# Block-sparse attention in 64-query blocks, with probabilities as weights of v and a planned order of all engines

## The chip, the cores and the metric

The kernel runs on one core of a Trainium2 chip. The metric is the device time of one launch in microseconds (us); lower is better. Engines are named as in the profile: PE is the matrix engine (PEld its weight loads), DVE the vector engine, ACT the scalar engine, POOL the GpSimd engine that issues the loads, SP the engine that issues the stores. PE reads from the on-chip memory and writes only to PSUM, which has eight banks of 512 float32 columns on 128 partitions; ACT and DVE move results out of it.

## The reference

Two parts follow each other. The first is attention over q, k and v of shape (4 batches, 8 heads, 768 positions, 64). Each query sees the keys less than 16 positions away, and besides them 24 summaries: for each block of 32 keys the elementwise maximum of k, with the mean of v as its value and log 32 added to its score.

```
scores_l = scale * q @ k^T          # kept where |i - j| < 16
scores_s = scale * q @ k_sum^T + log(32)
a = softmax([scores_l, scores_s]);  attn = a @ [v, v_sum]
```

The second part is a feed-forward network on the 3072 rows of the heads joined (512 wide): `h = x @ w_in` (512 to 2048), `g = h * clip(h + 3, 0, 6) / 6`, `out = g @ w_out` (2048 to 512). Inputs and output are float32; both kernels convert inputs to bf16 on load.

## The kernel before

**Tiles.** The 3072 rows are cut into eight tiles of 384 rows: half of a batch each. Heads are taken in four pairs p. For each tile, `F1` (L382) makes one 128-wide slice of h: four matmuls of 384 columns into the PSUM tile `hp` (L389), a Relu on ACT with the bias tile `half_c` (L392) and a DVE operation that makes `g` (L393); there are 16 slices. `F2` (L395) accumulates 16 matmuls of 512 columns per 128 rows (L402), copies the result on ACT (L406) and stores it from SP (L408).

**Attention by pair.** `Tk` and `Tq` (L264, L298) transpose k and q. Batches 0 and 1 are loaded as runs of eight rows (four for batch 0's q) and transposed by matmuls with a 64-wide output on half of the columns of the array (L271, L312); batches 2 and 3 come in natural order and take six 128-wide transposes per pair (L274, L305). Copies spread k into the block-diagonal tile `kbd` (two heads at once, 64 keys of each). `Sl` (L316) makes scores for 12 key blocks, each against 94 queries (L321), with Exp on ACT (L324) and a mask multiplication on DVE (L325). `Ss` (L327) makes the scores of the summaries (L331, L334). `AV` (L348) multiplies by v with the probabilities as the moving operand (L357, L359), makes the denominators with four more matmuls against a matrix of ones (L363 to L373), takes the reciprocal as Ln and Exp on ACT (L375, L376) and multiplies on DVE (L377); its result is already the transposed x that F1 reads. The block means of v come from an own load of v in float32, `vr`, added up on DVE (`vsum`, L229); for batch 0 from matmuls `vps` (L252) and a transfer `vs` on SP (L259).

**What sets the order.** POOL issues the loads in program order. Up to the first `AV`s of batch 0, PE, ACT and DVE also follow the program. Afterwards a table of slots (L451 to L501) puts the pieces of attention between the slices of the feed-forward part: one slot is one slice of F1 and three matmuls of F2 of the tile before. The work list (L503) runs F1 of tile 0 alone, then F1(1) with F2(0), F2(1) alone, F1(2) alone, F1(t) with F2(t-1) for t from 3 to 7, and F2(7) alone. The loads of batch 1 are held back until slice 11 of tile 0 exists (L490). PSUM: two banks each for `h`, `o` and `s`, and one each for `num` and `den`.

Of the kernel before, what the change touches and what calls it, by code (L numbers as in the profile page):

```python
# [14 lines left out]
ET = mybir.EngineType  # L15
# [3 lines left out]
KB = 64  # L19
HALO = 15  # L20
WIN = KB + 2 * HALO
HALF = 384
NLONG = 2
RUN = 8
PCS = 4
RP = 96
QCUT = 480
# [3 lines left out]
def kernel(  # L31
# [13 lines left out]
    NT = S // 128  # L45
    NK = S // KB
# [5 lines left out]
    RS = 4 * NB  # L52
# [3 lines left out]
    work = ctx.enter_context(tc.tile_pool(name="work", bufs=2))  # L56
    xp = ctx.enter_context(tc.tile_pool(name="xp", bufs=4))
    gp = ctx.enter_context(tc.tile_pool(name="gp", bufs=3))
    hw = ctx.enter_context(tc.tile_pool(name="hw", bufs=3))
    PS = bass.MemoryType.PSUM  # L60
    ps_h = ctx.enter_context(tc.tile_pool(name="ps_h", bufs=2, space=PS))
    ps_o = ctx.enter_context(tc.tile_pool(name="ps_o", bufs=2, space=PS))
    ps_s = ctx.enter_context(tc.tile_pool(name="ps_s", bufs=2, space=PS))
    ps_n = ctx.enter_context(tc.tile_pool(name="ps_n", bufs=1, space=PS))

    nc.scalar.preload_act_table_set("natural_log_exp_and_others")


    kbd = [const.tile([128, NK, 128], BF16, tag=f"kbd{p}", name=f"kbd{p}") for p in range(NP)]
    vall = const.tile([128, NP, NK, 128], BF16, tag="vbd", name="vbd")  # L70
    vbd = [vall[:, p] for p in range(NP)]
    qT = [const.tile([128, S + 2 * HALO + 2], BF16, tag=f"qT{p}", name=f"qT{p}") for p in range(NP)]
    at = [const.tile([128, NK, WIN], BF16, tag=f"at{p}", name=f"at{p}") for p in range(NP)]
    kst = [const.tile([128, RS], BF16, tag=f"kst{p}", name=f"kst{p}") for p in range(NP)]
    vst = [const.tile([RS, 2, D], BF16, tag=f"vst{p}", name=f"vst{p}") for p in range(NP)]
    w_in_sb = const.tile([128, NP, d_ff], BF16, tag="win", name="win")
    w_out_sb = const.tile([128, NFT, d_model], BF16, tag="wout", name="wout")


    kb_t, qb_t, vr_t, vf = {}, {}, {}, {}  # L80

    def load_k(b, p, n=1):

        if b < NLONG:
            t = ld.tile([RP, 2 * n, RUN, D], BF16, tag=f"kb{n}", name="kb", bufs=2)
            nc.gpsimd.dma_start(out=t[:], in_=k[b, 2 * p:2 * p + 2 * n].rearrange("h (p s) d -> p h s d", s=RUN))
        else:
            t = ld.tile([128, NT, 2, D], BF16, tag="kb", name="kb")
            load_natural(t, k, b, p)
        for i in range(n):  # L90
            kb_t[b, p + i] = t, i

    def load_q(b, p, n=1, part=None):

        if b < NLONG:
            lo, hi, r = cut(part)
            t = ld.tile([(hi - lo) // r, 2 * n, r, D], BF16, tag=f"qb{n}", name="qb", bufs=1 if n == 4 else 2)
            nc.gpsimd.dma_start(
                out=t[:], in_=q[b, 2 * p:2 * p + 2 * n, lo:hi].rearrange("h (p s) d -> p h s d", s=r))
        else:  # L100
            t = ld.tile([128, NT, 2, D], BF16, tag="qb", name="qb")
            load_natural(t, q, b, p)
        for i in range(n):
            qb_t[b, p + i, part] = t, i

    def cut(part):
        return {None: (0, S, RUN), 0: (0, QCUT, RUN // 2), 1: (QCUT, S, RUN // 2)}[part]

    def load_natural(t, src, b, p):
        for j in range(2):  # L110
            nc.gpsimd.dma_start(out=t[:, :, j], in_=src[b, 2 * p + j].rearrange("(s p) d -> p s d", p=128))  # L111

    def load_v(b, g, lo=0, hi=NK):

        for p in (2 * g, 2 * g + 1):
            for j in range(2):
                rows = slice(64 * j, 64 * j + 64)
                nc.gpsimd.dma_start(out=vall[rows, p, lo:hi, rows],  # L118
                                    in_=v[b, 2 * p + j].rearrange("(n k) d -> k n d", k=KB)[:, lo:hi])

    def load_vf(p):

        if not vf:
            t = gp.tile([128, NP, NK, D], F32, tag="g", name="vf")
            vf.update({i: t[:, i] for i in range(NP)})
        for j in range(2):
            nc.gpsimd.dma_start(out=vf[p][64 * j:64 * j + 64],  # L127
                                in_=v[0, 2 * p + j].rearrange("(n k) d -> k n d", k=KB))

    def load_vrows(b, g):  # L130

        w = BLK // PCS * D
        vr_t[b, g] = ld.tile([RS, PCS, w + 8], F32, tag="vr", name="vr", bufs=2)
        nc.gpsimd.dma_start(out=vr_t[b, g][:, :, 0:w],
                            in_=v[b, 4 * g:4 * g + 4].rearrange("h (n c t) d -> (h n) c (t d)", c=PCS, n=NB))

# [3 lines left out]
    def load_w_in(c):  # L140
        w = d_ff // 4
        nc.gpsimd.dma_start(out=w_in_sb[:, :, c * w:(c + 1) * w], in_=w_in_v[:, :, c * w:(c + 1) * w])

    def load_w_out(c):
        w = NFT // 4
        nc.gpsimd.dma_start(out=w_out_sb[:, c * w:(c + 1) * w], in_=w_out_v[:, c * w:(c + 1) * w])


    ctx.enter_context(tc.manual_schedule(engines={ET.Pool}))
    start = tc.manual_schedule(engines={ET.PE, ET.Activation, ET.DVE})  # L150
    start.__enter__()
    load_vf(0)
    ident = const.tile([128, 128], BF16, tag="id", name="ident")
    nc.gpsimd.memset(ident[:], 1.0)
    nc.gpsimd.affine_select(out=ident[:], in_=ident[:], compare_op=ALU.is_equal, fill=0.0, base=0,
                            channel_multiplier=1, pattern=[[-1, 128]])
    load_vf(1)
    load_k(0, 0)
    load_q(0, 0, 1, 0)
    load_vf(2)  # L160


    mask = const.tile([128, WIN], BF16, tag="mask", name="mask")
    nc.gpsimd.memset(mask[:], 1.0)
    for j in range(2):
        m = mask[j * 64:(j + 1) * 64]
        nc.gpsimd.affine_select(out=m, in_=m, compare_op=ALU.is_ge, fill=0.0, base=0,
                                channel_multiplier=-1, pattern=[[1, WIN]])
        nc.gpsimd.affine_select(out=m, in_=m, compare_op=ALU.is_ge, fill=0.0, base=2 * HALO,
                                channel_multiplier=1, pattern=[[-1, WIN]])  # L170
    load_vf(3)
    load_k(0, 1)
    load_q(0, 1, 1, 0)
    load_k(0, 2, 2)
    load_q(0, 2, 2, 0)


    hm4 = const.tile([RS, 4, D], F32, tag="hm4", name="hm4")
    osum4 = const.tile([RS, 4, D], BF16, tag="osum4", name="osum4")
    nc.gpsimd.memset(hm4[:], 1.0)  # L180
    nc.gpsimd.affine_select(out=hm4[:], in_=hm4[:], compare_op=ALU.is_ge, fill=0.0, base=0,
                            channel_multiplier=1, pattern=[[-NB, 4], [0, D]])
    nc.gpsimd.affine_select(out=hm4[:], in_=hm4[:], compare_op=ALU.is_ge, fill=0.0, base=NB - 1,
                            channel_multiplier=-1, pattern=[[NB, 4], [0, D]])
    hmv = [hm4[:, 2 * par:2 * par + 2] for par in range(2)]
    osum = [osum4[:, 2 * par:2 * par + 2] for par in range(2)]
    obd = const.tile([128, 2, D], BF16, tag="obd", name="obd")
    hmk = const.tile([128, 2, NB], BF16, tag="hmk", name="hmk")
    half_c = const.tile([128, 1], F32, tag="half", name="half_c")
    zero = const.tile([128, 1], F32, tag="zero", name="zero")  # L190
    nc.vector.memset(zero[:], 0.0)

    def zero_off_diagonal(eng, t):
        w = t.rearrange("p n c -> p (n c)").bitcast(F32).rearrange("p (n c) -> p n c", c=64)
        for r, c in ((slice(0, 64), slice(32, 64)), (slice(64, 128), slice(0, 32))):
            if eng is nc.scalar:
                eng.copy(w[r, :, c], zero[r].unsqueeze(2).to_broadcast([64, NK, 32]))
            else:
                eng.memset(w[r, :, c], 0.0)


    ind = const.tile([128, 2, 2, 4], F32, tag="ind", name="ind")
    nc.vector.memset(ind[:], 0.0)
    for i in range(4):
        for par in range(2):
            nc.vector.memset(ind[32 * i:32 * i + 32, par, par, i:i + 1], 1.0)
    for p in range(NP):
        zero_off_diagonal(nc.vector if p < 2 else nc.scalar, kbd[p][:])
    NK0 = 7
    load_w_in(0)  # L210

    def zero_rest():
# [4 lines left out]
        for t in (hmk, obd):  # L217
            nc.vector.memset(t[:], 0.0)
            nc.vector.memset(t[0:64, 0], 1.0)
            nc.vector.memset(t[64:128, 1], 1.0)  # L220
# [324 lines left out]
```

## Time and profile before

| | |
|---|---|
| median of three runs (lowest, highest) | 266.62 us (264.75, 266.89) |
| span of the profiled execution, first to last instruction | 262.8 us |
| what lies outside that span, against the median | 3.8 us |
| busy PE, ACT, DVE, POOL | 238.0, 169.3, 154.2, 72.5 us |
| first matmul of F1; last matmul of F2 | 34.85 us; 258.77 us |
| mean granted PE clock | 0.973 |

The profile is of one execution. For that execution it gives the span alone; its time is taken as the span and the 3.8 us that separate it from the median. A row of a group gives busy time and the mean of one instruction; the duration of a matmul contains a latency that overlaps with the next one, so the pace of matmuls is read from the distance of starts in the timeline or in the chain.

### The profile page before, as it was taken

The page shows a single profiled execution, that of the slowest core. Times are in us where ns is not written, and L with a number is a line of the kernel's source. Part 1 is how long each engine was busy: PE and PEld are TensorE (multiplying, and loading weights), DVE is VectorE, ACT ScalarE, POOL GpSimd, SP SyncE. Part 2 cuts the span into 40 slices and gives each one's busy share as a digit, 9 for nine tenths or more (in the row PEclk, how much of TensorE's full clock was granted, in tenths as well). Part 3 has the DMA queues.
Part 4 walks back from the last instruction along what each step waited for, and adds up shares of the span by engine and source line. Part 5 has one row for each costly group of instructions (what it writes and reads, how often), then busy time and mean ns, then how long its engine had stood idle before and what let it go on. Part 6 is the DMA issues. An engine that isn't in the chain of part 4 may idle for free.

```text
span 262.8 us, 4842 instructions
## 1 busy us (share of the span) xinstructions
PE 238.0 (91%) x1848; PEld 135.9 (52%) x1872; DVE 154.2 (59%) x360; ACT 169.3 (64%) x327; POOL 72.5 (28%) x104
## 2 busy tenths in 40 slices
PE   0946899999899969999899999999999999999993
PEld 0215556644455636666455556566655555555541
DVE  3594556632889774998994566668534544444400
ACT  7665578842587867998586567757766555555410
POOL 8994000566273600796920310000000000000000
PEclk9995599999999999999999999999999999999999
DMA  3999994299999971899990551001011111101122
GB/s 111 178 155 201 206 206 76 37 204 209 203 255 118 180 80 44 58 130 187 185 145 19 54 70 44 36 7 40 2 40 40 42 40 40 40 2 41 40 82 80
DMA packets 57848, 25.80 MB, mean 98 GB/s; under 512 B 45281, under 2 KB 53217, under 8 KB 57825
## 3 DMA queue, kind: packets, MB, share of 16 engines
q0 software_dynamic: 54160, 19.14, 63.5%
q1 hardware_dynamic: 3664, 6.34, 6.5%
q8 instruction: 15, 0.25, 0.4%
q14 instruction: 9, 0.07, 0.1%
HBM read 31.98 MB, written 6.29 MB: 146 GB/s over the span
## 4 chain that ended last, share of the span: by engine, by line
PE 62%; DMA 11%; DVE 8%; ACT 7%; POOL 7%; issue 3%; ACTq 0%; POOLq 0%
PE op L402 24%; PE hp L389 24%; DMA vr<-in_v_dram 8%; POOL vbd L118 3%; PE num L359 2%; DMA vs<-vs 2%; PE sl L321 2%; POOL vf L127 2%; DVE g L393 2%; PE num L357 2%; PE ss L331 2%; ACT kbd L281 2%; PE den L363 1%; PE den L366 1%; DMA vf<-in_v_dram 1%
## 5 line engine op out<-in xcount | busy, mean ns | idle before, releaser
L389 PE MATMUL hp<-x,win 128*128 128x384 bf16 x512 | 104.1, 326 | 2.8 <-DVE g L393 2.4
L392 ACT ACTIVATE r<-hp,half_c 128x384 f32<-128x384 f32 x128 | 73.5, 580 | 45.8 <-PE hp L389 45.0
L402 PE MATMUL op<-wout,g 128*128 128x512 bf16 x360 | 96.2, 379 | 1.1 <-issue 0.2
L393 DVE SCALAR_TENSOR_TENSOR g<-r,hp 128x384 bf16<-128x384 f32 x128 | 69.6, 551 | 45.6 <-ACT r L392 45.4
L389 PEld LDWEIGHTS <-win 128*128 128x128 bf16 x512 | 47.3, 98 | 37.2 <-issue 6.0
L402 PEld LDWEIGHTS <-g 128*128 128x128 bf16 x384 | 36.8, 98 | 32.8 <-issue 0.5
L377 DVE TENSOR_TENSOR x<-num,lg 128x384 bf16<-128x384 f32 x32 | 17.7, 555 | 24.7 <-ACT lg L376 22.8
L118 POOL DMA_DIRECT2D vbd<-in_v_dram x24 | 18.2, 775 | 37.7 <-PE num L359 33.6
L375 ACT ACTIVATE lg<-den 128x384 f32<-128x384 f32 x32 | 15.7, 492 | 16.0 <-PE den L373 7.4
L324 ACT ACTIVATE at<-sl 128x376 bf16<-128x376 f32 (+2 forms) x48 | 22.4, 490 | 2.3 <-PE sl L321 2.3
L406 ACT COPY ot<-op 128x512 f32<-128x512 f32 x24 | 13.9, 583 | 8.9 <-PE op L402 8.8
L325 DVE TENSOR_TENSOR at<-at,mask 128x376 bf16<-128x376 bf16 (+2 forms) x48 | 16.2, 349 | 3.6 <-ACT at L324 3.4
L359 PEld LDWEIGHTS <-vbd 128*128 128x128 bf16 x224 | 13.8, 102 | 8.0 <-issue 4.5
L376 ACT ACTIVATE lg<-lg 128x384 f32<-128x384 f32 x32 | 16.8, 526 | 0.8
L321 PE MATMUL sl<-qT,kbd 128*128 128x94 bf16 x192 | 15.0, 214 | 1.9 <-ACT at L324 0.8
L321 PEld LDWEIGHTS <-kbd 128*128 128x128 bf16 x192 | 12.2, 102 | 7.7 <-issue 1.8
L359 PE MATMUL num<-at,vbd 128*128 128x94 bf16 (+2 forms) x224 | 15.0, 206 | 0.0
L111 POOL DMA_DIRECT2D qb<-in_q_dram x16 | 13.5, 861 | 4.8 <-DMA vr<-in_v_dram 4.8
L252 PE MATMUL vps<-vf,ind 128*8 128x384 f32 x16 | 7.5, 612 | 7.6 <-DMA vf<-in_v_dram 7.6
L111 POOL DMA_DIRECT2D kb<-in_k_dram x16 | 13.5, 865 | 0.0
L357 PE MATMUL num<-asum,vst 96*128 96x384 bf16 x32 | 11.0, 344 | 2.6 <-DVE x L377 2.2
L281 ACT COPY kbd<-tp 64x768 bf16<-64x768 bf16 x12 | 9.5, 792 | 5.2 <-PE tp L271 5.1
(82 smaller groups left out, 219.8 us busy)
## 6 DMA issues: line engine op xcount, KB each, us to landing
out_dram<-ot SPq DMA_DIRECT2D x24, 256.0 KB, 2.0
vr<-in_v_dram POOLq DMA_DIRECT2D x6, 768.0 KB, 7.7
vbd<-in_v_dram POOLq DMA_DIRECT2D x24, 96.0 KB, 3.9
win<-in_moe_w_in_dram POOLq DMA_DIRECT2D x4, 512.0 KB, 11.1
wout<-in_moe_w_out_dram POOLq DMA_DIRECT2D x4, 512.0 KB, 18.3
vf<-in_v_dram POOLq DMA_DIRECT2D x8, 192.0 KB, 3.7
kb<-in_k_dram POOLq DMA_DIRECT2D x16, 96.0 KB, 6.8
qb<-in_q_dram POOLq DMA_DIRECT2D x16, 96.0 KB, 6.4
```

Of the source, the lines that this page charges most:

```text
L111: nc.gpsimd.dma_start(out=t[:, :, j], in_=src[b, 2 * p + j].rearrange("(s p) d -> p s d", p=128))
L118: nc.gpsimd.dma_start(out=vall[rows, p, lo:hi, rows], in_=v[b, 2 * p + j].rearrange("(n k) d -> k n d", k=KB)[:, lo:hi])
L321: nc.tensor.matmul(sp[:, i * WIN:(i + 1) * WIN], kbd[p][:, t], qT[p][:, t * KB:t * KB + WIN], start=True, stop=True)
L324: nc.scalar.activation(a, sp[:, 0:n * WIN].rearrange("p (n c) -> p n c", c=WIN), AF.Exp, scale=scl)
L357: nc.tensor.matmul(num[:], vst[p][:].rearrange("p h d -> p (h d)"), asm[:], start=True, stop=False)
L359: nc.tensor.matmul(num[:, lo:hi], vbd[p][:, t], a[:, t, off:off + hi - lo], start=False, stop=(i == len(bl) - 1))
L376: nc.scalar.activation(lg[:], lg[:], AF.Exp, scale=-1.0)
L377: nc.vector.tensor_tensor(xt[s][:, p], num[:], lg[:], op=ALU.mult)
L389: nc.tensor.matmul(hp[:], w_in_sb[:, kt, ft * 128:(ft + 1) * 128], xt[t][:, kt], start=(kt == 0), stop=(kt == NP - 1))
L392: nc.scalar.activation(r[:], hp[:], AF.Relu, bias=half_c[:], scale=1.0 / 6.0)
L393: nc.vector.scalar_tensor_tensor(gt[t][:, ft], r[:], 1.0, hp[:], op0=ALU.min, op1=ALU.mult)
L402: nc.tensor.matmul(op[:], gt[t][:, ft, ts * 128:(ts + 1) * 128], w_out_sb[:, ft], start=(ft == 0), stop=(ft == NFT - 1))
```

## The change

The attention part is written anew; the feed-forward part keeps its matmuls. By parts:

- **Scores.** A query block has 64 queries. Its keys stand in one tile `kaug` of 120 columns: 64 own keys, 16 to the right, 16 to the left, and 24 maxima. For each head, one matmul with 64 rows of weights (the head's 64 features, on partitions 0 to 63 or 64 to 127) makes the scores of all 120 keys against 64 queries: 12 matmuls per pair and half batch, the two heads into two banks of the PSUM tile `S` (new L378 to L396). One Exp over 120 x 768 and one mask multiplication over 96 x 768 follow.
- **Values.** The probabilities of 64 queries become the weights (120 rows, 64 columns), and `vaug` moves: 64 values and a column that holds 1 for keys and 32 for summaries, so that the 65th output is the denominator. The two query blocks of 128 rows go to output partitions 0 to 63 and 64 to 127: 16 matmuls of 65 columns per 128 rows (new L433). DVE takes a reciprocal and scales; four 128-wide transposes and one ACT copy make x.
- **Loads.** k and q come as runs of eight and four rows for every batch (four heads per load), and are transposed as batches 0 and 1 were before. v comes in bf16 with 64 rows per block; its 16-row edges come from two more loads per half for batches 1 to 3 and from copies on DVE for batch 0. The `vr` loads and their DVE sums are gone: matmuls against an indicator (128 columns, 32-wide output) make the block sums, which eight transfers on SP per batch spread into `vaug` (batch 0: ACT and DVE copies).
- **Feed-forward.** The Relu takes its bias 0.5 as a number, not as a tile. The first three slices of tile 0 are split by 128 rows. F1(t) runs with F2(t-1) in every stage; F2 accumulates four matmuls at a time. The last 128 rows are done in two halves of 256 columns.
- **PSUM.** Three banks `h`, one `o`, two for the one tile `S` (scores and values share it), two `T` (all transposes and block sums).
- **Order.** Each piece is an `Op` with an engine, a cost in us, what it reads and writes, and a priority. `Plan.run` simulates the five engines, always starts the operation of the best priority among those that can start within 0.12 us of the earliest, and its list is the order of every engine.

The core of the diff:

```diff
-ld = ctx.enter_context(tc.tile_pool(name="ld", bufs=4))
-ps_h ... ps_o ... ps_s ... ps_n
+plan = Plan({"h": [3 banks], "o": [1 bank], "S": [one tile of 2 banks], "T": [2 banks],
+             "g": 3, "x": 4, "xn": 3, "r": 4, "rc": 3, "red": 3, "vs": 2, "ot": 3})
...
+            for i in range(HQ):
+                t = half * HQ + i
+                for j in range(2):
+                    rows = slice(64 * j, 64 * j + 64)
+                    nc.tensor.matmul(X.slot[:, j, i * QB:(i + 1) * QB], kaug[p][rows, t], qT[p][rows, t * QB:(t + 1) * QB],
+                                     start=True, stop=True)
...
+                for h in (2 * p, 2 * p + 1):
+                    for c in range(2):
+                        t = 2 * T + c
+                        nc.tensor.matmul(o[64 * c:64 * c + 64, h % 4], at[p][0:KEYS, h % 2, t * QB:(t + 1) * QB],
+                                         vaug[i][0:KEYS, h, t, 0:D + 1], start=True, stop=True)
...
+                nc.vector.reciprocal(r, src[..., D])
+                nc.vector.tensor_tensor(o, src[..., 0:D], r.unsqueeze(len(r.shape)).to_broadcast(list(o.shape)), op=ALU.mult)
...
-        nc.scalar.activation(r[:], hp[:], AF.Relu, bias=half_c[:], scale=1.0 / 6.0)
+        nc.scalar.activation(r.slot[:], h.slot[:, 0:HALF], AF.Relu, bias=0.5, scale=1.0 / 6.0)
...
+    for g in range(2):
+        load_k(0, g, -100 + 2 * g)
+        load_q(0, g, 0, -99 + 2 * g)
+    const_ops()
+    for c in range(NP):
+        load_v(0, c, -80 + c)
+    load_w(0, -40)
+    load_w(1, -38)
...
+    for p in range(NP):
+        k_step(0, p, -90 + 4 * p, ("ACT", "ACT"), bank="h", late=30)
+        q_step(0, p, 0, -88 + 4 * p, "ACT")
+        scores(0, p, 0, -86 + 4 * p)
+        vsum_first(p, -60 + p, ("ACT", "DVE"), -30 + p)
+        halo(p, ("DVE", "DVE"), -60 + p)
...
+    for o in plan.run():
+        o.fn()
```

Per batch from 1 on there are then, as pieces on PE: four transposes of k and four of q (16 matmuls each), eight scores, six values, six transposes of x, and one block sum of v.

More of the change, by code (lines that the diff above doesn't have):

```diff
@@ L71 @@
[L71 to L77, printed above, removed]
@@ L80 @@
[L80 to L104, printed above, removed]
@@ L106, in cut @@
[L106 to L135, printed above, removed]
+    ps = ctx.enter_context(tc.tile_pool(name="ps", bufs=1, space=bass.MemoryType.PSUM))
@@ L145, in load_w_out, with load_w2 @@
+    def load_w2(c, prio):
         w = NFT // 4
[L146 to L199, printed above, removed]
@@ L202 @@
[L202 to L212, printed above, removed]
-        for p in range(NP):
-            nc.vector.memset(qT[p][:, 0:HALO], 0.0)
-            nc.vector.memset(qT[p][:, S + HALO:], 0.0)
-            nc.vector.memset(kst[p][:], 0.0)
[L217 to L220, printed above, removed]
-        nc.vector.memset(half_c[:], 0.5)
@@ L262, with copy @@
-    asum = {}
-    def Tk(b, p):
-        pool, tag = (ps_o, "o") if b == 0 else (ps_s, "s")
-        tp = pool.tile([128, S], BF16, tag=tag, name="tp")
-        (t, i), long = kb_t[b, p], b < NLONG
-        if long:
+        op("POOL", 0.8, lambda: nc.gpsimd.dma_start(out=w_out_sb[:, c * w:(c + 1) * w], in_=w_out_v[:, c * w:(c + 1) * w]),
+           w=[("wout", c)], prio=prio, dma=2.6)
+    def copy(eng, o, i):
+        {"ACT": nc.scalar.copy, "DVE": nc.vector.tensor_copy, "POOL": nc.gpsimd.tensor_copy}[eng](o, i)
@@ L275, in Tk @@
-        red = work.tile([128, NB], BF16, tag="red", name="red")
-        for j in range(2):
-            copy = nc.scalar.copy if j == 0 or (b < 2 and p % 2 == 1) else nc.vector.tensor_copy
-            rows = slice(64 * j, 64 * j + 64)
-            o = kbd[p][rows, :, 64 * j:64 * j + 64]
-            if long:
-                copy(o.rearrange("p n (c s) -> p n c s", s=RUN), tp[rows].rearrange("p (s n c) -> p n c s", s=RUN, n=NK))
-            else:
-                copy(o, tp[rows].rearrange("p (n c) -> p n c", c=KB))
@@ L327, in Ss @@
-    def Ss(b, g, half):
-        sp = ps_s.tile([128, 512], F32, tag="s", name="ss")
-        for par in range(2):
-            p = 2 * g + par
-            nc.tensor.matmul(sp[0:RS, 0:HALF], kst[p][:], qT[p][:, HALO + half * HALF:HALO + (half + 1) * HALF],
-                             start=(par == 0), stop=(par == 1))
-        a = work.tile([RS, HALF], BF16, tag="asum", name="asum", bufs=4)
-        nc.scalar.activation(a[:], sp[0:RS, 0:HALF], AF.Exp, scale=scl)
-        asum[b, g, half] = a
@@ new lines, in values @@
+        groups = [[p] for p in range(NP)] if by_pair else [[0, 1], [2, 3]] if banks else [list(range(NP))]
+        for n, ps_ in enumerate(groups):
+            x = X[ps_[0] // 2] if banks else X[0]
+            new = ps_[0] % 2 == 0 if banks else n == 0
+            op("PE", mm(4 * len(ps_), D) / 2 + 0.05, lambda ps_=ps_: mms(ps_), r=[("at", p, half) for p in (range(NP) if n == 0 else ps_)]
+               + [(m, i, p) for p in ps_ for m in ("v", "vl", "vr")] + [("vsum", i, p, half) for p in ps_], w=[x],
+               prio=prio, alloc=x if new else None)
```

660 lines of the change are left out of this document (415 added, 245 removed).

## The prediction

> **What bounds the kernel now.** I read the page first (busy shares and the 40 slices), then the windows, then the chain of waits, then PE's timeline.
>
> ```profile
> span 262.8 us, 4842 instructions
> ...
> PE 238.0 (91%) x1848; PEld 135.9 (52%) x1872; DVE 154.2 (59%) x360; ACT 169.3 (64%) x327; POOL 72.5 (28%) x104
> ...
> PE   0946899999899969999899999999999999999993
> ...
> PEclk9995599999999999999999999999999999999999
> ```
>
> PE is full from the sixth slice on (a slice is 6.57 us); ACT and DVE have a third of their time free. The only long hole is the start. The next rows cut the span at the starts of F1's tiles; columns are stretch, length, busy time with instruction counts, granted clock, DMA share, GB/s. First all engines, then F1's line L389, then F2's L402, whose weight loads are counted completely (96 = two tiles).
>
> ```profile
> 0.00:34.85 34.85, 21.19 (x193) 11.00 (x193) 19.07 (x72) 22.66 (x41) 21.12 (x37) 0.80 1.00 172
> 34.85:101.70 66.85, 62.17 (x557) 34.94 (x562) 43.34 (x95) 46.59 (x93) 24.85 (x33) 1.00 1.15 148
> ...
> 151.83:206.72 54.89, 54.38 (x418) 32.76 (x424) 33.23 (x69) 37.53 (x75) 0.36 (x1) 1.00 0.14 34
> 206.72:227.48 20.76, 20.66 (x111) 10.97 (x112) 9.32 (x17) 10.97 (x20) 0.00 (x0) 1.00 0.10 38
> ...
> 258.77:262.80 4.03, 0.00 (x0) 0.00 (x0) 0.00 (x0) 0.59 (x1) 0.00 (x0) 0.95 0.17 65
> ```
>
> ```profile
> 34.85:101.70 66.85, 25.70 (x129) 11.78 (x129) 1.00 1.15 148
> 101.70:151.83 50.13, 26.29 (x128) 11.46 (x129) 1.00 1.18 107
> 151.83:206.72 54.89, 26.03 (x128) 11.63 (x128) 1.00 0.14 34
> 206.72:227.48 20.76, 13.02 (x64) 6.27 (x64) 1.00 0.10 38
> ```
>
> ```profile
> 34.85:101.70 66.85, 24.16 (x89) 8.66 (x96) 1.00 1.15 148
> 101.70:151.83 50.13, 11.89 (x43) 4.70 (x48) 1.00 1.18 107
> 151.83:206.72 54.89, 24.42 (x90) 9.35 (x96) 1.00 0.14 34
> ```
>
> From the chain, in the stretch without attention (start, length, what):
>
> ```profile
> 219.86 0.65 PE hp L389 x4
> 220.51 0.65 PE op L402 x3
> ```
>
> So a matmul of F1 costs 0.1625 us and one of F2 0.2165; 512 and 384 of them are 83.2 + 83.1 = 166.3 us, and 64 + 48 are 20.8, the whole stretch from 206.72. The rest of the span is 96.5 us: 34.85 before the first F1, 4.03 at the end, and what attention adds. In 151.83:206.72 that is 54.89 - 2 x 20.8 = 13.3 us for one batch (batch 3); in 101.70:151.83, with 128 + 48 matmuls (31.2 us), 18.9 for batch 2; in 34.85:101.70 (128 + 96, 41.6 us) 25.3 for batch 1 and the second half of batch 0. The work of batches 2 and 3 is the same, so 5.6 us of batch 2 are stalls, and about as much of the first stretch.
>
> **The change, part by part.** *Feed-forward:* same columns, 166.3 us. The split slices (36 matmuls of 128 columns for 12 of 384) and the halves of the last rows move no column; I set them to nothing, as matmuls here cost by columns, and they run where PE is full or at the end.
>
> *Transposes of k and q.* They now take the form of batches 0 and 1 everywhere. PE's timeline of batch 1 between matmuls of F2, and short pieces between F1s (start, length with latency):
>
> ```profile
> 64.74 1.24 PE L402 MATMUL op<-wout,g 128*128 128x512 bf16 x5
> 65.92 0.53 PE L271 MATMUL tp<-ident,kb 96*64 96x96 bf16 x16
> 66.38 0.39 PE L402 MATMUL op<-wout,g 128*128 128x512 bf16 x1
> ```
>
> ```profile
> 39.51 0.37 PE L321 MATMUL sl<-qT,kbd 128*128 128x94 bf16 x5
> 39.72 0.82 PE L389 MATMUL hp<-x,win 128*128 128x384 bf16 x4
> 40.47 0.32 PE L312 MATMUL tp<-ident,qb 72*64 72x72 bf16 x8
> 40.72 0.82 PE L389 MATMUL hp<-x,win 128*128 128x384 bf16 x4
> ```
>
> Five of F2 from 64.74 end at 65.82; the transposes start 0.10 later, and the next F2 comes 0.46 after them. An excursion of 16 costs 0.56 us: about 0.095 to enter, as much to leave, and 0.37 for eight pairs (0.046 a pair, both halves of the columns at once). Eight per batch: 4.5 us. A q half of batch 0: 39.72 + 0.65 = 40.37 to 40.72, so 0.35.
>
> *Scores.* The five L321 take 0.21 us, 0.042 each for 94 columns, or 0.029 for 64. No row shows weights on 64 rows. Lower end: two heads at once at 0.029 a pair, 6 x 0.029 = 0.17; upper end: one after another at 0.042, 0.50; entering and leaving 0 to 0.19. Nearest is the pair of L271 (0.046): I take 0.27 + 0.19 = 0.46, eight per batch 3.7. That a row tile pays for entering like a column tile is my choice, by the nearest row, the entry of L271. The Trainium skill, "TensorEngine Tiling (Array Packing)", Key Properties, says that a change of tiling mode, not just of tile, drains the engine, which the 0.10 before the transposes bears out for column tiles; by that rule all scores pay, and without it the 32 scores would be 6 us cheaper together.
>
> *Values.* 16 matmuls of 65 columns on the two column halves, the form nearest to L271: 0.23 (0.029 a pair) to 0.67 (16 x 0.042); I take 0.31 + 0.19 = 0.50, six per batch 3.0. Four transposes of x of 128 columns at 0.056 (0.042 x 128/94): 0.225, six per batch 1.35. Block sums: 48 matmuls of 128 columns, four at once 0.7 to one by one 2.7; I take 0.85 + 0.19 = 1.05. A batch: 4.5 + 3.7 + 3.0 + 1.35 + 1.05 = 13.6 us, against 13.3 now: PE's work does not fall. Three batches 40.8; the second half of batch 0 has four q (1.4), four scores (1.85), three values (1.5), three x (0.65): 5.4.
>
> *ACT and DVE.*
>
> ```profile
> L392 ACT ACTIVATE r<-hp,half_c 128x384 f32<-128x384 f32 x128 | 73.5, 580 | 45.8 <-PE hp L389 45.0
> L393 DVE SCALAR_TENSOR_TENSOR g<-r,hp 128x384 bf16<-128x384 f32 x128 | 69.6, 551 | 45.6 <-ACT r L392 45.4
> ...
> L324 ACT ACTIVATE at<-sl 128x376 bf16<-128x376 f32 x40 | 19.0, 491 | 1.8 <-PE sl L321 1.8
> ...
> L377 DVE TENSOR_TENSOR x<-num,lg 128x384 bf16<-128x384 f32 x32 | 17.7, 555 | 24.7 <-ACT lg L376 22.8
> L376 ACT ACTIVATE lg<-lg 128x384 f32<-128x384 f32 x32 | 16.8, 526 | 0.8
> L375 ACT ACTIVATE lg<-den 128x384 f32<-128x384 f32 x32 | 15.7, 492 | 16.0 <-PE den L373 7.4 <-PE den L370 7.2 <-DVE x L377 0.6
> ...
> L281 ACT COPY kbd<-tp 64x768 bf16<-64x768 bf16 x12 | 9.5, 792 | 5.2 <-PE tp L271 5.1
> ...
> L285 DVE TENSOR_REDUCE red<-tp 128x24 bf16<-128x768 bf16 x8 | 7.6, 954 | 0.9 <-ACT kbd L281 0.8
> ```
>
> ACT loses Ln and Exp of the denominators (64, 32.5 us) and Relu's tile operand (Ln of the same size is 0.09 shorter: 0 to 11.5 us, no row says it is the operand). It gains longer Exps (32 x 0.81, from 491 ns for 376 and about 0.83 ns a column), 24 copies of x (0.6, L375 and 128 columns more) and q copies of 768 columns (0.8, as L281): near 150 us. DVE loses L377 and the sums of vr, and gains a reciprocal and a 512-wide scaling per 128 rows (24 x 0.8, L377 and a third more) and second halves of k: near 155. A batch puts 36 to 39 us on each (ACT: 32 Relus 15.7 to 18.6, eight Exps 6.5, twelve copies of 0.6, k and q 6.3) while PE does 41.6 + 13.6 = 55; so they hide. Where the cover is thin is tile 0: F1 alone gives PE 10.4 us, with 5.4 of attention, and ACT has 16 Relus (8 to 9), 3.4 of put-off k copies and 6.7 for half a batch: about 19. That costs 3 us, counted under stalls.
>
> *Loads and queues.* In POOL's list the start is k, q (four loads), constants, four loads of v, then weights.
>
> From the timeline, then the chain, then the groups:
>
> ```profile
> 5.03 0.67 POOL L86 DMA_DIRECT2D kb<-in_k_dram  x1
> 5.67 0.97 POOL L98 DMA_DIRECT2D qb<-in_q_dram  x1
> ...
> 8.77 0.47 POOL L169 TENSOR_SCALAR_AFFINE_SELECT mask<-mask 64x94 bf16<-64x94 bf16 x1
> ...
> 10.57 0.40 PEld L271 LDWEIGHTS <-kb 96*64 96x64 bf16 x16 [0.64 <-issue]
> 10.58 0.53 PE L271 MATMUL tp<-ident,kb 96*64 96x96 bf16 x16
> ```
>
> ```profile
> 18.04 6.23 DMA vs<-vs
> ```
>
> ```profile
> L118 POOL DMA_DIRECT2D vbd<-in_v_dram x24 | 18.2, 775 | 37.7 <-PE num L359 33.6 <-ACT r L392 2.0 <-PE hp L389 1.6
> ```
>
> Now k comes after two loads of v, its transposes begin at 10.6, and the chain goes through a 6.2 us transfer `vs`. In the new order four issues of 0.7 to 1.0 from about 1.3 us on end at 4.5, seven constant operations (0.2 to 0.5 each, as L169) at 7, four loads of v (each twice L118's rows, 1.5) and three more constants at 15. From the issue of k to its first transpose were 5.5 us (5.03 to 10.57), so k is there at 6.5 to 9 and v at 17 to 19. Those loads hold 1.97 MB in bf16, 11.5 us at the first row's 172 GB/s: the issues set the time, not the bytes. Then a block sum, its spreading copy (0.8), values, scaling (0.8), transposes and copy (0.9): the first F1 at 22, dense F1 at about 24. ACT (four pairs of two k copies, q, Exp: 8 us) and DVE (four of reduce, maxima, mask and edges: 15 us) have the time from 7 on. Lower end 21, upper end today's 34.85. w_in's chunks follow v at 3 us each, as fast as F1 uses them (4 slices 2.6 us). The eight spreading transfers per batch wait on SP for the DVE copy of the sums, with stores queued behind them (three `ot` buffers cover those); `vs` took 6.2 us here, and the priorities leave seven slots, some ten us, before the values need them.
>
> *End.* 4.03 now; the last copy is half as wide, 0.2 less, which I leave out.
>
> *Sum.* 24 + 166.3 + 5.4 + 40.8 + 4.0 = 240.5. Stalls: at least those of batch 3 now, about 1 us per batch; at most 5.6 per batch and 3 in tile 0, 20. The order is fixed for all engines, PE cannot pass a piece whose Exp is late, and one `S` and one `o` leave no second buffer; I take 8, as F2 lies in every stage to cover. Span 248.5; the median lies 3.8 above the span now, so 252.3 us.
>
> **Rivals.** (1) *The start stays*: dense F1 at 33 to 35, as DVE's edge copies or v come late: 262. For it: the DMA share of the first row is 1.00, and the clock in slices 4 and 5 is 0.5. Against it: the 6.2 us transfer is gone. (2) *The small matmuls do not overlap* (other side): scores 0.50, values 0.67, block sum 2.7 and the switches make a batch 19.4 us instead of 13.6, three of them +17.4, half of batch 0 and the start +4: 274. It decides from +14.3 us, that is about 20 ns more per small matmul. Against it: L271's 16 in 0.37 us; for it: no row has weights on 64 rows or 120 x 64. (3) *Weight loads set the pace of the values*: in the row of L271, 16 loads of 64 columns last 0.40 us in all, so 0.025 each. If they stood alone at 0.1 each, a value step would be 1.6 instead of 0.31, 24 of them +31: 283. The same 16 in 0.40 speak against it. The Trainium skill, "TensorEngine Tiling (Array Packing)", Restrictions, has the rule: column tiling switches Fast Weight Load off; with the 64/1.2 = 53 ns of "TensorE: Matmul & The Clock Gate", LDWEIGHTS, an estimate is 0.85 a step and 265. By the 25 ns the trace does not bear it out. (4) *The listed order stalls*: an Exp or a copy later than planned holds PE, and with it every other engine's list. Above 22 us of stalls nothing is gained; the first stretch has 5.5 in 67 us with two banks each of `o` and `s`, and twice that rate over 215 us is 35: 279.
>
> **How the numbers follow.** Runs spread by 0.8%, so 1% (264.0 to 269.3) is about what can be told from no change. Forecast 0.66 (own range 243 to 262), (1) 0.14, (2) 0.06, (3) 0.02, (4) 0.12. Faster: 0.65 of the forecast, 0.10 of (1), 0.01 of (4), 0.76; same: 0.01, 0.04 of (1), 0.03 of (4), 0.08; slower: (2), (3) and 0.08 of (4), 0.16. Below 243 lies 0.06 (start 21, pairs at 0.029, stalls 4: 242), above 270 (2), (3) and 0.06 of (4), 0.14; range 243 to 270.
>
> **What would show it.** First F1 near 22 to 25 (right) or past 30 (wrong). From PE's timeline, a score step near 0.46 and a value step near 0.50 from the end of the F1 before to the start of the next, and L271's successor at 0.56. Batches 2 and 3 at 13 to 15 us beyond 41.6. Relu at 490 or 580 ns. If batches cost 19, (2) or (4): the idle columns of PE, behind ACT or DVE, tell which.

## The result, and the profile after

| | before | after |
|---|---|---|
| median (lowest to highest, four runs each) | 266.28 us (264.75 to 266.89) | 254.17 us (250.17 to 255.64) |
| ratio after to before, 95% interval | | 0.946 (0.937 to 0.954) |
| profiled execution: time, span | span 262.8 us | 253.56 us, span 251.9 us |
| first matmul of F1 | 34.85 us | 32.57 us |
| busy PE, ACT, DVE, POOL | 238.0, 169.3, 154.2, 72.5 us | 226.4, 139.6, 145.8, 49.6 us |

Ratios leave out runs that lie more than 1.5% above the fastest of the same kernel (two of the four of after); the profiled executions of e2 and e9 are such runs, so their waits and spans are those of a slower execution.

By the medians of all runs the changed kernel is 12.1 us faster: 254.2 us where 252.3 (243 to 270) was forecast. In its page, the same lines as before:

```profile
span 251.9 us, 6009 instructions
...
PE 226.4 (90%) x2475; PEld 132.0 (52%) x2504; DVE 145.8 (58%) x319; ACT 139.6 (55%) x277; POOL 49.6 (20%) x74
...
PE   0762899999985999999999999999999999999994
...
PEclk9999999999996799999999999999999999999999
```

PE has two holes: the start (the `2` in the fourth slice), and slice 13 (the `5`, 75.6 to 81.9 us), with a lower clock in slices 13 and 14. The windows at the starts of F1's tiles, columns as in the windows shown of before:

```profile
0.00:32.57 32.57, 17.09 (x289) 14.98 (x289) 22.21 (x57) 16.53 (x38) 20.29 (x36) 1.00 1.49 166
...
55.09:89.36 34.27, 29.93 (x397) 17.02 (x400) 18.68 (x43) 19.45 (x37) 8.07 (x11) 0.90 1.47 117
89.36:113.65 24.29, 24.08 (x318) 13.58 (x320) 16.19 (x36) 15.80 (x32) 8.63 (x11) 1.00 1.75 105
...
248.20:251.90 3.70, 0.02 (x1) 0.00 (x0) 0.00 (x0) 0.37 (x1) 0.00 (x0) 1.00 0.12 40
sum 251.90, PE 226.41 PEld 131.95 DVE 145.75 ACT 139.59 POOL 49.58; mean PE 22.64 PEld 13.20 DVE 14.58 ACT 13.96 POOL 4.96
```

Between the first F1 and the last matmul lie 251.90 - 32.57 - 3.70 = 215.6 us, of which PE is busy for 226.41 - 17.09 - 0.02 = 209.3 and idle for 6.3. Before, the same windows (34.85 to 258.77) add up to 223.9 us, with PE busy for 216.8 and idle for 7.1. The feed-forward part is put at 166.3 in both (after's chain has the same pace, eight matmuls of F1 in 1.30 us and eight of F2 in 1.73); PE's attention therefore fell from 50.5 to 43.0 us, and what happens to the clock is part of the 43.0. So the 10.9 us of the span are 2.3 at the start, 8.3 in the middle and 0.3 at the end.

**The start.** From the timeline of after, PE, DVE and ACT (in brackets: idle time before, and what ended it):

```profile
24.08 1.84 DVE L315 CAST vaug<-T 24x768 bf16<-24x768 f32 x2
25.10 2.72 PE L403 MATMUL T<-vaug,ind 64*32 64x128 bf16 x24 [3.60 <-DVE vaug L315]
26.57 0.79 ACT L315 CAST vaug<-T 24x768 bf16<-24x768 f32 x1 [4.89 <-PE T L403]
...
32.57 1.61 PE L504 MATMUL h<-x,win 128*128 128x128 bf16 x18
```

The block sums of pairs 2 and 3 (L403) wait 3.6 us for a `T` bank. Both banks still hold the sums of pairs 0 and 1, whose second copy into `vaug` stands in DVE's list behind the edge copies and the first scalings. ACT meanwhile waits 4.9 us for these sums.

**The hole at 75 us.** PE's timeline of after, then PE's windows there (busy, clock, DMA share, GB/s), then SP's queue, then the transfer in the chain of waits:

```profile
74.64 0.26 PE L449 MATMUL S<-vaug,at 120*64 120x65 bf16 x4
75.82 0.22 PE L449 MATMUL S<-vaug,at 120*64 120x65 bf16 x2 [0.92 <-DMA vaug<-vs]
76.86 0.22 PE L449 MATMUL S<-vaug,at 120*64 120x65 bf16 x2 [0.82 <-DMA vaug<-vs]
77.97 0.27 PE L449 MATMUL S<-vaug,at 120*64 120x65 bf16 x2 [0.89 <-DMA vaug<-vs]
79.07 0.78 PE L449 MATMUL S<-vaug,at 120*64 120x65 bf16 x6 [0.83 <-DMA vaug<-vs]
```

```profile
75.00:80.00 5.00, 1.56 (x13) 0.78 0.50 67
80.00:85.00 5.00, 4.78 (x45) 0.53 0.11 42
85.00:90.00 5.00, 4.84 (x54) 1.00 0.03 10
```

```profile
66.07 8.69 SPq L427 DMA_DIRECT2D vaug<-vs  x8
```

```profile
72.82 6.56 DMA vaug<-vs
```

The first values of batch 1 take their summaries from eight transfers that SP issues one after another, 1.09 us each. The one that PE waits for last was issued at 72.82 and landed 6.56 us later, at 79.38: 13.3 us after the first issue. PE reaches the first values 8.6 us after the first issue and then goes at the pace at which transfers land, one step of two matmuls per 1.1 us: it idles for 3.5 us of the 4.2 between 74.9 and 79.1. Over the window from 80 to 85 us the granted clock is 0.53, which costs 4.78 x 0.47 = 2.2 us more.

### The profile page after: what moved, and what is told of

It reads as the page before. It is cut to its first block, busy times and chain, and to the rows that moved or that the text cites. A ratio compares the mean times of both kernels' runs of the same rounds, so it can differ in the third digit from the quotient of the medians.

```text
span 251.9 us, 6009 instructions
## 1 busy us (share of the span) xinstructions
PE 226.4 (90%) x2475; PEld 132.0 (52%) x2504; DVE 145.8 (58%) x319; ACT 139.6 (55%) x277; POOL 49.6 (20%) x74
## 4 chain that ended last, share of the span: by engine, by line
PE 81%; DVE 5%; ACT 4%; DMA 3%; SPq 2%; issue 2%; POOL 2%; POOLq 0%; ACTq 0%
PE h L504 34%; PE o L523 27%; PE h L523 4%; PE S L449 3%; PE S L386 3%; PE T L484 3%; DMA vaug<-vs 3%; SPq L427 2%; PE T L327 2%; PE T L369 2%; PE T L403 2%; DVE red L349 2%; DVE vaug L315 1%; ACT kaug L315 1%; PE T L419 1%
## 5 line engine op out<-in xcount | busy, mean ns | idle before, releaser
L504 PE MATMUL h<-x,win 128*128 128x384 bf16 (+1 forms) x536 | 99.7, 323 | 0.2 <-DVE g L511 0.2
L509 ACT ACTIVATE r<-h 128x384 f32<-128x384 f32 x128 | 62.6, 494 | 54.3 <-PE h L504 46.0
L511 DVE SCALAR_TENSOR_TENSOR g<-r,h 128x384 bf16<-128x384 f32 x128 | 69.4, 551 | 39.5 <-ACT r L509 37.6
L523 PE MATMUL o<-wout,g 128*128 128x512 bf16 x308 | 82.0, 382 | 2.0 <-issue 0.9
L394 DVE TENSOR_TENSOR at<-at,mask 96x768 bf16<-96x768 bf16 x32 | 17.7, 554 | 23.8 <-ACT at L391 23.1
L391 ACT ACTIVATE at<-S 120x768 bf16<-120x768 f32 x32 | 26.2, 818 | 5.4 <-PE S L386 5.4
L276 POOL DMA_DIRECT2D vaug<-in_v_dram x16 | 15.3, 957 | 33.0 <-PE S L449 26.2
L488 ACT COPY x<-T 128x512 bf16<-128x512 bf16 x24 | 13.9, 584 | 5.5 <-PE T L484 5.5
L315 ACT COPY qT<-T 128x768 bf16<-128x768 bf16 (+1 forms) x20 | 13.1, 680 | 5.6 <-PE T L369 5.6
L475 DVE TENSOR_TENSOR xn<-S,rc 128x512 bf16<-128x512 f32 x22 | 15.2, 690 | 0.6
L265 POOL DMA_DIRECT2D qnat<-in_q_dram x16 | 10.9, 684 | 9.4 <-DMA win<-in_moe_w_in_dram 3.4
```

What stands on the lines that cost most here:

```text
L276: op("POOL", 1.5, lambda: nc.gpsimd.dma_start(out=o[0:QB, lo:hi, 0:D], in_=rows[:, lo:hi]), w=[("v", b % 2, c)], prio=prio, dma=2.0)
L315: {"ACT": nc.scalar.copy, "DVE": nc.vector.tensor_copy, "POOL": nc.gpsimd.tensor_copy}[eng](o, i)
L391: op("ACT", act(2 * HALF), lambda: nc.scalar.activation(a, X.slot[0:KEYS, :, 0:HALF], AF.Exp, scale=scl), r=[X], w=[("at", p, half)], prio ...
L394: op("DVE", dve(2 * HALF, 1.92), lambda: nc.vector.tensor_tensor(m, m, mask[:, half * HQ:(half + 1) * HQ].unsqueeze(1).to_broadcast([WIN, ...
L475: nc.vector.tensor_tensor(o, src[..., 0:D], r.unsqueeze(len(r.shape)).to_broadcast(list(o.shape)), op=ALU.mult)
L504: nc.tensor.matmul(h.slot[:, lo * 128:hi * 128], w_in_sb[:, kt, ft * 128:(ft + 1) * 128], xt[s].slot[:, kt, lo * 128:hi * 128], start=(kt ...
```

## The experiments

The question: which of the two holes holds the time, why is the second there, and why was PE's attention cheaper than priced? The theory was that each hole costs its whole length, so that filling it shortens the run by its length. The rival was that time won ahead of a wait set by DMA is lost in that wait.

**e1: the start alone.** The second copies of the sums go to ACT and right behind the first.

```diff
-        vsum_first(p, -60 + p, ("ACT", "DVE"), -30 + p)
+        vsum_first(p, -60 + p, ("ACT", "ACT"), -60 + p)
```

> Theory A (the start of the changed kernel waits for the T banks of the block sums, which the second spreading copies hold, as these stand on DVE behind the edge copies of v): with those copies on ACT at once, PE's wait of 3.6 us before the third block sum goes, first F1 at 28.5 instead of 32.6, span some 248. Rival B (the start is set by the arrival of v, or by DVE's edge copies themselves): the block sums come earlier or not, but the first F1 stays within 1 us of 32.6.

Measured: 253.44 us, ratio to before 0.956 (0.952 to 0.960): no gain over after that can be told. Its first F1 starts at 27.20, 5.4 us earlier, so the reason for the late start is right. PE's timeline of e1:

```profile
27.20 1.44 PE L504 MATMUL h<-x,win 128*128 128x128 bf16 x12
...
69.83 0.65 PE L504 MATMUL h<-x,win 128*128 128x384 bf16 x3
73.70 0.22 PE L449 MATMUL S<-vaug,at 120*64 120x65 bf16 x2 [3.22 <-DMA vaug<-in_v_dram]
74.78 0.22 PE L449 MATMUL S<-vaug,at 120*64 120x65 bf16 x2 [0.86 <-DMA vaug<-vs]
```

PE reaches the first values at 70.5 instead of 74.6, but their data come as late as before (SP issues at 65.73, for 8.25 us): the marked waits there are 7.0 us, twice those of after. The profile puts the first of them down to a load of v, but batch 1's last load of v was issued at 49.68 and none of these loads took more than 15.3 us to land; SP's first transfer is what is left. What was won at the start was handed back at the next wait set by DMA. The rival holds.

**e4: another way to an earlier start.** Batch 0's edges come by four loads instead of eight DVE copies.

```diff
+    for g in range(2):
+        load_vhalo(0, g, -76 + g)
...
-        halo(p, ("DVE", "DVE"), -60 + p)
```

> The edges of batch 0's v by four more loads instead of eight DVE copies (5 us of DVE). If DVE's copies hold the start (rival of e1), the first F1 comes 3 to 5 us earlier than 32.6; if only the place of the spreading copies does, the gain is that of 2 to 4 us by which they move up, with w_in 3 us later and not needed before. If the loads of v set it, the first F1 moves later by 1 to 3 us, as 3072 more packets stand before w_in.

Measured: 256.19 us, ratio 0.967 (0.962 to 0.972). The first F1 came at 29.16, 3.4 us earlier, so the edge copies have a part in the late start. But the block sum of batch 1 ran at 71.13 instead of 64.26, and PE waited 5.2 us for `vaug<-vs` between 76 and 83 us: the gain was lost at the same wait.

**e2 and e3: the wait alone, and both.** Batch 1's sums are spread by copies from `T` on ACT and DVE in turn, as for batch 0, without SP's transfers; e3 adds e1.

```diff
+        if copies:
+            for c in range(NP):
+                eng = ("ACT", "DVE")[c % 2]
...
+                    copy(eng, vaug[i][WIN:KEYS, 2 * c:2 * c + 2, :, 0:D],
+                         T.slot[32 * c:32 * c + NB, 0:2 * D].rearrange(...).unsqueeze(2).to_broadcast(...))
...
-        vsum(b, base + 10)
+        vsum(b, base + 10, b == 1)
```

> In the changed kernel PE waits 4.6 us near 75 to 79 us for the eight transfers that spread batch 1's block sums, and its clock then drops to 0.53 for 5 us. Theory A (the eight issues on SP, 1.1 us each, set that wait): with batch 1's sums spread by two copies on ACT and two on DVE the wait and the drop go, 4.6 + 2.4 us, span near 245. Rival B (v or the probabilities of batch 1 are late anyway, so that the next wait stands at the same place): a wait of 3 us or more stays there, span 249 or more.

> Both edits. If the two waits are independent, the gains add: first F1 near 28.5, no wait at the first values of batch 1, span some 241. If the loads of batch 1 set its values (rival), an earlier start only lengthens the wait there: span 245 or more.

Measured: e2 255.36 us, ratio 0.962 (0.957 to 0.967); e3 251.18 us, 0.947 (0.942 to 0.951). The wait for `vaug<-vs` of batch 1 is gone, but e2's timeline shows what came in its place:

```profile
66.31 1.43 ACT L315 CAST vaug<-T 24x1536 bf16<-24x1536 f32 x1
...
67.78 1.75 DVE L315 CAST vaug<-T 24x1536 bf16<-24x1536 f32 x1 [0.90 <-ACT vaug L315]
...
69.56 1.43 ACT L315 CAST vaug<-T 24x1536 bf16<-24x1536 f32 x1 [1.00 <-DVE vaug L315]
...
71.03 1.76 DVE L315 CAST vaug<-T 24x1536 bf16<-24x1536 f32 x1 [1.50 <-ACT vaug L315]
71.71 0.82 ACT L391 ACTIVATE at<-S 120x768 bf16<-120x768 f32 x1
...
72.58 0.35 PE L386 MATMUL S<-qT,kaug 64*128 64x64 bf16 x12 [2.99 <-ACT at L391]
```

The four copies run one after another, each waiting for the one before, though they read different partitions, write different columns and stand on two engines: 6.5 us in all. An Exp waits behind them in ACT's list, and PE 3 us for the Exp. The experiment replaced one wait by another of its own: e2 is no faster than after, and e3 gains only 2.3 us over e1. It does not tell what filling the hole is worth; the next ones do.

**e8: sums earlier.** On top of e1, the block sum of a batch gets a better priority (`base + 1` for `base + 10`), and the loads of v a lower cost in the plan.

> With e1's edit, and the plan told that v's loads take half as long (they were there at 57 us, the block sum of batch 1 ran at 64) and that the sum comes first. Theory A (the eight transfers on SP start late and take 8 to 13 us): the sum runs near 58 to 60, the wait at batch 1's first values shrinks from 7.0 us to 3 or less, span 246 to 248. Rival B (v's arrival sets it): the sum cannot run earlier than 64 and the wait stays near 7, span 252.

Measured: 256.58 us, ratio 0.965 (0.961 to 0.969). The sum ran at 58.92, so v's arrival does not set it. SP issues from 60.15 on, 5.6 us earlier than in e1, but takes 10.0 us for the eight, and the planner, which knows nothing of this, moved the values forward as well: the marked waits are 7.6 us, where e1 has 7.0. The theory missed; that the planner's belief makes the hole is what the next experiment tries.

**e9: the true cost in the plan.** On top of e1, only two numbers change. The plan had a pair of these transfers at 0.1 us on SP and 1.0 us to land.

```diff
-            op("SP", 0.1, spread, r=[vs], w=[...], prio=prio + 0.2, dma=1.0)
+            op("SP", 2.1, spread, r=[vs], w=[...], prio=prio + 0.2, dma=3.0)
```

> With e1's edit, and the plan told what the transfers cost (2.1 us per pair on SP instead of 0.1, and 3.0 to land instead of 1.0); nothing is made faster. Theory (the wait is a wrong cost in the plan, for work of F2 was there to be done meanwhile): the plan puts 16 matmuls of F2 ahead of the values, the 7.0 us wait and the drop of the clock behind it go, span 243 to 246. Rival (PE has no other work ready at that place): the wait only moves, span 250 or more.

Measured: 242.73 to 243.18 us in the three runs of the ratio, 246.76 to 248.69 in the other three, 244.97 as the median of all; ratio 0.913 (0.910 to 0.916), the lowest here. The first F1 stays at 27.20. SP's queue and the only long wait of PE behind the first F1 in e9's profile, which is that of the run of 246.76 us:

```profile
65.22 8.55 SPq L427 DMA_DIRECT2D vaug<-vs  x8
```

```profile
78.45 0.51 PE L449 MATMUL S<-vaug,at 120*64 120x65 bf16 x12
80.97 0.27 PE L449 MATMUL S<-vaug,at 120*64 120x65 bf16 x2 [2.01 <-DMA vaug<-vs]
```

The transfers go out at the same time and as slowly as in e1; the values now come 8 us later, with F2 matmuls in between. One wait of 2.0 us is left of 7.0. With the hole covered, the start's gain reaches the end. The two numbers hold for the transfers of batches 2 and 3 too, so other pieces may have moved as well; the run does not separate them.

**e10: faster transfers.** On top of e1, the loads of batch 2 are held by a small POOL copy that reads the last column the transfers of batch 1 write; the plan keeps the wrong cost.

```diff
+        if b == 2:
+            op("POOL", 0.2, lambda: nc.gpsimd.tensor_copy(pace[...], vaug[1][..., H - 1, NQ - 1, 0:2]),
+               r=[("vsum", 1, NP - 1, 1)], w=["pace"], prio=base - 20)
```

> With e1's edit, and batch 2's loads held until batch 1's last transfer on SP has landed. If the transfers are slow because they share the DMA engines with batch 2's loads, they take 2 us less from issue to landing or more and the wait of 7.0 us falls to 3 to 5; if SP's issues (1.1 us each) set them, they take the 8 us as before and the wait stays at 6 to 7. In both cases batch 2 starts later, which may cost as much.

Measured: 248.66 us, ratio 0.933 (0.931 to 0.936). SP's queue and PE's waits in e10:

```profile
64.79 6.75 SPq L432 DMA_DIRECT2D vaug<-vs  x8
```

```profile
70.69 0.22 PE L454 MATMUL S<-vaug,at 120*64 120x65 bf16 x2 [0.78 <-DMA vaug<-vs]
...
72.19 0.22 PE L454 MATMUL S<-vaug,at 120*64 120x65 bf16 x2 [0.63 <-DMA vaug<-vs]
73.02 0.26 PE L454 MATMUL S<-vaug,at 120*64 120x65 bf16 x2 [0.60 <-DMA vaug<-vs]
```

Without the loads beside them the eight issues take 6.75 us, not 8.25, and above all the data land sooner: in the chains the transfer that PE waits for last takes 2.21 us from issue to landing here and 7.25 in e1. The marked waits fall from 7.0 us to 2.4. So the hole had two causes, the wrong cost in the plan and the loads of batch 2 beside the transfers. How the loads slow them, by the DMA engines' time or otherwise, was not tried apart.

**e11 and e12: the two together with others.** e11 is e8 with e9's cost, e12 is e10 with e9's cost.

> The edits of e1, e8 and e9 together. If all three theories hold, no wait of over 1 us is left between the first F1 (27) and the end: 27 + 166 + 42 + 1 + 4, span 240 to 243. If the loads bound the first half, the waits move to another place and the span stays at 245 or more.

> The edits of e1, e9 and e10 together: the plan knows the transfers' cost, and batch 2's loads don't share the DMA engines with them. If both theories hold, no wait of over 1 us stands at batch 1's values, the clock stays full, and the span is 240 to 242 in every run, as in the runs of e9 without a wait. If the held loads of batch 2 come too late (rival), PE waits for k or q of batch 2 near 85 us and the span is 244 or more.

Measured: e11 246.09 us, ratio 0.923 (0.920 to 0.927); e12 245.19 us, 0.922 (0.918 to 0.926). By the ratio neither beats e9, and both miss the span of 240 to 243 us that was expected of them. In e12 no wait for `vaug<-vs` is left, the issues take 6.75 us, and its six runs lie between 244.87 and 245.50 us, where e9's spread from 242.73 to 248.69. So the two gains do not add. Part of what e12 lost can be read: while F2 runs alone (74 to 79 us), PE waits twice 0.67 us for ACT's copy out of the one `o` bank; in e9 transposes of batch 2's k and a block sum stand there, for which e12's held loads come too late. The rest, and e11's lag, stay open.

**e6 and e7: the price of changing the array's form.** One extra matmul of 64 columns precedes each of the 16 slices of F1 of tile 7, where no attention is left: with 64 rows of weights in e6, with 128 in e7. Its result is overwritten.

```diff
+            if s == NTILE - 1:
+                nc.tensor.matmul(h.slot[:, 0:64], w_in_sb[0:64, 0, ...], xt[s].slot[0:64, 0, 0:64], start=True, stop=True)
```

> The changed kernel with one more matmul ahead of each of the 16 slices of F1 of tile 7: 64 rows of weights, 64 columns, overwritten by the slice. If entering and leaving row tiles costs 0.19 us as for column tiles, each slice of that stage starts 0.22 us later, 3.5 us in all over a stretch without attention; if a row tile is entered freely, 0.03 each, 0.5 us in all.

> The same extra matmul with all 128 rows, so without a change of tiling: 0.03 us each by both theories, 0.5 us in all. The difference of the two runs in that stage is the price of the change of tiling.

Each ran once (e6 256.18 us, e7 251.93), so the price is read within the profile, at a granted clock of 1.00. From the start of the first whole slice of tile 7 to its last matmul of F1 the plain kernel takes 19.73 us, e7 20.18 and e6 23.32; 15 of the 16 extra matmuls lie in between. One slice each, e6 and then e7:

```profile
221.07 0.81 PE L526 MATMUL o<-wout,g 128*128 128x512 bf16 x3
221.81 0.20 PE L504 MATMUL h<-x,win 64*128 64x64 bf16 x1
221.94 0.82 PE L507 MATMUL h<-x,win 128*128 128x384 bf16 x4
```

```profile
222.34 0.19 PE L504 MATMUL h<-x,win 128*128 128x64 bf16 x1
222.37 0.81 PE L507 MATMUL h<-x,win 128*128 128x384 bf16 x4
```

A matmul of 64 columns costs 0.45/15 = 0.03 us in the same form, and 3.59/15 = 0.24 with 64 rows. The pair of changes costs 0.21 us: 0.09 in (221.07 + 0.65 = 221.72 to 221.81), and the rest out. The price that the forecast took from column tiles, 2 x 0.095, holds within 0.02 us for row tiles.

**e5: the Relu's operand alone.** The kernel before, with `bias=0.5` for the tile.

> The kernel before with one part of the change alone: Relu's bias as a number. If the operand costs, Relu falls from 580 to about 490 ns and ACT's busy time by 11 us. Theory (PE bounds the stretch with F1): the time stays within 1% of before, at most 1 us less. Rival (ACT's length sets stalls of PE): 3 us or more less.

Measured: 265.76 us, ratio 1.003 (0.998 to 1.007). The group of the Relu in e5:

```profile
L392 ACT ACTIVATE r<-hp 128x384 f32<-128x384 f32 x128 | 62.1, 489 | 52.6 <-PE hp L389 50.6
```

580 ns became 489: the tile operand was the whole difference. ACT gets 11 us of free time, and the kernel nothing, since PE waited for ACT for only 1.6 us in all in the kernel before.

## Why the prediction came out right

The median was hit to 1.9 us, by luck: errors of up to 8.6 us cancel. The table takes the profiled run of 253.56 us.

| term (us) | predicted | measured | difference |
|---|---|---|---|
| start, to the first F1 at full pace | 24 | 32.6 | +8.6 |
| feed-forward, by its pace | 166.3 | 166.3 | 0 |
| PE's attention after the start, at full clock | 46.2 | 43.0 - 2.2 = 40.8 | -5.4 |
| stalls: PE idle, and the low clock | 8 | 6.3 + 2.2 = 8.5 | +0.5 |
| end | 4.0 | 3.7 | -0.3 |
| outside the span | 3.8 | 1.7 | -2.1 |
| sum | 252.3 | 253.6 | +1.3 |

**The start failed.** By the forecast's own sign (22 to 25 right, past 30 wrong) the first F1 at 32.57 speaks against it. The step put the first F1 at 22 and counted the work of DVE and ACT as if each could run in any order. It left out that a bank of `T` is held until its second reader is through, and that this reader stands late in DVE's list. Rival (1) happened, though neither by v nor by the edge copies alone: e1 leaves the edge copies on DVE and moves only the sums' second copies, and gains 5.4 us; e4 takes the edge copies away, and gains 3.4. The other 5.2 us (27.20 in e1, not 22) were not taken apart. e1's timeline shows what stands there: the sums of the four pairs start one by one (14.26, 16.65, 19.28 and 21.07), about 1.46 us each, with two copies of 0.8 us on ACT behind each, where the forecast added up one sum and one copy.

**PE's attention was priced too high, and that of before read too low.** PE's timeline of after, a score step and a value step between feed-forward matmuls:

```profile
70.10 0.81 PE L504 MATMUL h<-x,win 128*128 128x384 bf16 x4
70.84 0.35 PE L386 MATMUL S<-qT,kaug 64*128 64x64 bf16 x12
71.13 1.04 PE L523 MATMUL o<-wout,g 128*128 128x512 bf16 x4
...
127.18 0.81 PE L504 MATMUL h<-x,win 128*128 128x384 bf16 x4
127.93 0.44 PE L449 MATMUL S<-vaug,at 120*64 120x65 bf16 x16
128.30 1.04 PE L523 MATMUL o<-wout,g 128*128 128x512 bf16 x4
```

From the end of four F1 (70.75) to the next F2 a score step takes 0.38 us, not 0.46: with 0.21 of that for entering and leaving (e6), 12 matmuls take 0.17, 0.029 a pair. Two row tiles do run side by side, at the lower end of the range; the forecast took the pair of L271, whose matmuls have 96 columns. A value step takes 0.47 us (127.83 to 128.30), not 0.50. Sixteen loads of weights go into the 0.37 us from its first matmul to the next F2, 0.023 each, which ends rivals (2) and (3). Transposes and x came as priced. With a block sum of 0.8, a batch is 8 x 0.56 + 8 x 0.38 + 6 x 0.47 + 6 x 0.225 + 0.8 = 12.5 us instead of 13.6. Three batches and the half of batch 0 make 42.5 by these prices; the table's 40.8 counts PE's busy time, so the short gaps on entering and leaving stand there under idle time.

"PE's work does not fall" was wrong by more than that. The forecast called 5.6 of the 18.9 us of batch 2's stretch stalls, and about as much of the first stretch. The windows of before for all engines, and then for L357 alone (one per `AV`), say otherwise:

```profile
101.70:151.83 50.13, 48.45 (x424) 30.70 (x426) 39.80 (x92) 38.26 (x80) 26.18 (x34) 1.00 1.18 107
```

```profile
101.70:151.83 50.13, 3.93 (x12) 1.18 (x12) 1.00 1.18 107
151.83:206.72 54.89, 2.62 (x8) 0.79 (x8) 1.00 0.14 34
```

PE idles for 1.7 us there (and 4.7 in the first stretch), and the stretch has 12 `AV`s where batch 3's has 8: four belong to batch 1. PE's attention before was 50.5 us and its idle time 7.1, so the gain of the middle is fewer PE microseconds (50.5 to 40.8), not fewer stalls.

**Stalls: the size right, the shape wrong.** Not about a microsecond in every batch, but one hole (75 to 79 us) and the clock behind it. The step on SP's transfers is the one that failed here: it saw that seven slots, some ten us, are left before the values need them, and took that for enough. PE came 8.6 us after the first issue, but eight issues in a row took 8.7 us, and each transfer had yet to land: 6.56 us for the one that PE waited for last, much like the 6.2 of `vs` that the forecast had read. Issue and landing together are 13.3 us. e9 (the plan) and e10 (the loads beside them) show both parts. Beyond that hole the listed order kept PE fed, so rival (4) did not come.

**ACT, DVE and the Relu.** From the groups of after:

```profile
L509 ACT ACTIVATE r<-h 128x384 f32<-128x384 f32 x128 | 62.6, 494 | 54.3 <-PE h L504 46.0
...
L391 ACT ACTIVATE at<-S 120x768 bf16<-120x768 f32 x32 | 26.2, 818 | 5.4 <-PE S L386 5.4
...
L475 DVE TENSOR_TENSOR xn<-S,rc 128x512 bf16<-128x512 f32 x22 | 15.2, 690 | 0.6
```

Relu 494 ns, Exp 818 (0.81 was priced), scaling 690 with a reciprocal of 208 (0.8 was priced for both). They hide, as forecast, and ACT's 139.6 and DVE's 145.8 us lie 10 and 9 below it.

**Outside the span.** The forecast set the span of one execution against a median of others. Where time and span of the same execution are known, they differ by 1.7 us (253.56 and 251.9 in after, 245.17 and 243.5 in e12), so by an estimate the profiled execution of before took about 264.5 and not 266.6. That put 2.1 us too much on the sum.

## What to carry to other kernels

A gain ahead of a wait set by DMA comes out at the end only when that wait moves too: look for the next wait on the same path and price both. A planner's list is as good as its costs, and both the issue of a transfer on its queue, once for each transfer in a row, and its time to land beside other loads belong to them. Before calling a stretch's excess stalls, read PE's idle time in it and count whose pieces lie in it.

## What the runs showed of the hardware

- A change of the array's form has a price: about 0.21 us in and out for 64 rows (e6 against e7), 0.19 for the 64-column transposes. The Trainium skill, "TensorEngine Tiling (Array Packing)", Key Properties, says that a change of mode drains the engine; the trace agrees.
- The granted clock falls after thin work: 0.53 over 80 to 85 us, behind the hole of 75 to 79 us. It was 0.986 over the profiled run of after and 0.998 in that of 250.17 us, so part of the spread of after's runs is this. The Trainium skill, "TensorE: Matmul & The Clock Gate", What's actually happening, has half rate after one idle window of about 3.4 us; the 0.53 agrees. In e9 the clock was 0.66 in the window of 80 to 85 us behind a single wait of 2.0 us, which one such idle window doesn't explain.
- At the start of after the rows give a clock of 1.00, but the same shapes take longer there: twelve score matmuls 0.50 us at 31.31 and 0.35 at 35.41, a block-sum matmul 311 ns (L403) and later 214 (L419). It looks like the slow clock behind the hole, and the 1.00 of these first rows is not to be relied on; no run settles it.
- SP takes 0.84 us for one of these transfers in a row of eight without loads beside them (6.75/8 in e10), and 0.95 (7.62/8 in e4) to 1.25 (10.0/8 in e8) with them. From issue to landing the one waited for last took 2.2 us in e10, and 6.6, 7.25 and 8.6 in after, e1 and e9.
- Copies out of one PSUM bank on ACT and DVE, 1.43 to 1.76 us each, did not overlap (e2); whether the bank or the order made by the language forces that wasn't tried.
